# A quarter of the first product by Strassen's seven products in blocks 3 to 5 of a retention and PReLU kernel

## The chip, the cores and the metric

The kernel runs on one NeuronCore of one Trainium2 chip. The metric is the device time of one execution in microseconds. The core has five engines with a queue each: TensorE (PE in the profile, its weight loads PEld), VectorE (DVE), ScalarE (ACT), GpSimd (POOL) and SyncE (SP), which here only starts transfers. SBUF is the memory that all of them read; PSUM holds TensorE's results in eight banks of 128 x 512 fp32.

## The reference

Retention first: for 4 batches and 8 heads of width 64, over 768 positions, a state of 64 x 64 per head decays and takes up the outer product of key and value; the output is the query times the state. The outputs, as 3072 tokens of 512 features, then go through two products with a PReLU between them.

```python
gamma = 1.0 - 2.0 ** (-5.0 - np.arange(H))
for t in range(S):
    state = gamma[None, :, None, None] * state + np.einsum('bhd,bhe->bhde', k[:, :, t], v[:, :, t])
    y[:, :, t] = scale * np.einsum('bhd,bhde->bhe', q[:, :, t], state)
x = y.transpose(0, 2, 1, 3).reshape(B * S, H * D)     # 3072 x 512
h = x @ w_in                                          # 3072 x 2048, the first product
g = np.maximum(h, 0.0) + alpha * np.minimum(h, 0.0)
out = g @ w_out                                       # 3072 x 512, the second product
```

## The kernel before

**Units and blocks.** The positions are cut into 24 units of 128 (`NU`), six to a batch. A block is four units, 512 tokens (`TB`), and there are six blocks. The first eight units are handled as four double units by functions whose names begin with `u`; from unit 8 on the plain ones serve. For a unit, k and q are loaded (`load`, SyncE), scaled by powers of gamma to f16 (`scaled`, mostly GpSimd, L139), turned by a transposing transfer (`turn`, SyncE, L164), and v is cast (`cast`). `prep` does the four for one unit. Then TensorE makes `scores` (L236) and `states` (L196) of a pair of units, VectorE masks the scores (`masked`, L250) and sums the states (`sums`, L211 and L217, with a multiply on GpSimd, L219), and TensorE makes the outputs (`out_first`, `out_second`, L295), which ScalarE and VectorE copy to `xT`, the next block's tokens.

**The first product.** `ffn1` (L622) walks over 16 tiles of 128 of the 2048 hidden features. One tile is four matmuls of 128 weights by 512 tokens, k from the four quarters of the 512 features; `w_in_all` and `xT` lie in SBUF as f16. ScalarE takes the relu of the negated sum (`hm`, L631), VectorE adds the alpha part to PSUM's value (L632) and writes `gt`, the activated tile, in f16. `gt` is one buffer, `hps` takes the four banks p0 to p3 in turn. Blocks 0 and 1 use `ffn1_half` (L650, L659, L664) as well, half the tokens at a time.

**The second product.** Block 0 uses plain matmuls (`ffn2_start`, `ffn2`). From block 1 on, `seven` multiplies 2 x 2 quarters by Strassen's scheme in Winograd's form: seven products of 16 matmuls of 256 columns (L789), in the order A00, A01, `gs1`, `gs0`, `gs2`, A11, `gs3`. The sums of the weights are made once (`w_sums`). The sums of the activations are made per block by `g_sums(n, part, which, eng)` (L739), a subtraction or addition of 128 x 1024 f16 with both inputs and the output in SBUF; part 0 covers the first four tiles of each half of the features, part 1 the other four, and `which` runs from 0 to 3. They land in four tiles `gs0` to `gs3`, which block 0 uses as its `gt`. ScalarE keeps partial results (`kept`, L807), VectorE adds them to later ones (L819), SyncE stores.

**The order of the work** is written by hand: every engine runs its instructions in the order in which the program issues them, and waits on semaphores for inputs and for buffers. The two products are generators; `tick(gen, m)` lets m matmuls out, so that other work can be put between them. In a block n from 2 on, TensorE does `ffn1(n)`, scores and states of the next block's first pair, `seven(n)` with `T_OUT1` = 44 matmuls, the first pair's outputs and the second pair's scores and states, `T_OUT2` = 46 matmuls, the second pair's outputs, and the 22 matmuls that are left. GpSimd's `prep` of the next block's units is issued during `ffn1`, and runs as soon as its buffers (`kq`, four of them) are free. Block 1 has its own arrangement in the same loop (`n > 1` else), with `g_sums` of both parts on VectorE ahead of `seven`.

## Time and profile before

| what | value |
|---|---|
| median of three runs | 199.34 us (198.3, 199.36, 199.34) |
| the profiled execution | 198.51 us, of which its span is 196.5 us |
| granted clock of TensorE | full speed in all 40 slices |
| busy: TensorE, VectorE, GpSimd, ScalarE | 97%, 77%, 61%, 50% of the span |
| `ffn1` of a steady block | 13.81 us |
| last matmul to the end of the span | 3 us |

From 17 us to 193 us TensorE has work almost without a gap. The steady blocks are 28.9 us apart. In a timeline of one engine, a row gives start and duration in us (of several instructions together where a count stands behind the tiles), the engine, the line, the operation, output and inputs with shapes, and in brackets the idle time before it with what ended it. In the chain of work, a row is start, duration, engine, tile and line.

### The profile page before, as it was taken

Reading aid. Unit: us, or ns where it says so; the run is one execution under the profiler, and the core shown is the slowest. Engines: PE = TensorE matmul, PEld = TensorE weight load, DVE = VectorE, ACT = ScalarE, POOL = GpSimd, SP = SyncE. Lnnn points to the kernel's source line nnn. Section 1 sums busy time; section 2 is a strip of 40 time slices with the busy share of each in tenths; the row PEclk is TensorE's granted clock in tenths of the full one; section 3 lists DMA queues with packets and bytes.
Section 4 is the critical chain, followed back from the end, with each engine's and each line's share of the span. In section 5 each row is a group of like instructions: output and inputs, shape, how many; then the busy total and the mean of one; then the engine's idle time right before and its main releaser. Section 6 shows DMA issues by size and latency. Waiting matters only on the chain.

```text
span 196.5 us, 6280 instructions
## 1 busy us (share of the span) xinstructions
PE 190.3 (97%) x2632; PEld 128.9 (66%) x2632; DVE 151.1 (77%) x259; ACT 98.5 (50%) x192; POOL 119.8 (61%) x134
## 2 busy tenths in 40 slices
PE   7988999999999999999999999999999999999993
PEld 5757544558668888644888544888544888444882
DVE  2597989164989998589988589976689985789913
ACT  3378663238677925466333467234476234566110
POOL 3378989999999276994097992197971290040000
PEclk9999999999999999999999999999999999999999
DMA  5999999999998499999999999982660011300014
GB/s 157 330 358 389 407 388 329 337 332 206 209 226 188 89 291 219 226 295 257 213 228 208 286 171 251 253 208 78 180 141 0 3 57 55 109 0 3 0 53 160
DMA packets 92746, 38.75 MB, mean 197 GB/s; under 512 B 70176, under 2 KB 88624, under 8 KB 92720
## 3 DMA queue, kind: packets, MB, share of 16 engines
q1 hardware_dynamic: 91440, 37.36, 74.1%
q10 hardware_dynamic: 1280, 1.01, 1.6%
q8 instruction: 20, 0.33, 0.7%
q14 instruction: 6, 0.05, 0.1%
HBM read 27.35 MB, written 6.29 MB: 171 GB/s over the span
## 4 chain that ended last, share of the span: by engine, by line
PE 81%; DVE 9%; SPq 2%; DMA 2%; POOL 2%; issue 1%; ACT 1%; POOLq 0%
PE hps L622 33%; PE ops L789 28%; PE ops L717 5%; PE hps L650 5%; DVE gt L664 4%; SPq L342 2%; DMA qu<-in_q_dram 2%; DVE gs L739 2%; PE ops L686 2%; PE ya L524 1%; POOL gs L739 1%; PE ya L295 1%; DVE um L496 1%; PE yb L295 1%; PE sca L236 1%
## 5 line engine op out<-in xcount | busy, mean ns | idle before, releaser
L622 PE MATMUL hps<-xT,win 128*128 128x512 f16 x304 | 66.4, 379 | 0.0
L632 DVE SCALAR_TENSOR_TENSOR gt<-hm,small,hps 128x512 f16<-128x512 f32 x76 | 55.4, 745 | 8.6 <-ACT hm L631 3.5
L631 ACT ACTIVATE hm<-hps 128x512 f32<-128x512 f32 x76 | 45.4, 597 | 27.5 <-PE hps L622 27.5
L622 PEld LDWEIGHTS <-win 128*128 128x128 f16 x304 | 29.7, 98 | 34.8
L789 PEld LDWEIGHTS <-gs 128*128 128x128 f16 x320 | 30.9, 98 | 4.2 <-DVE gs L739 0.3
L139 POOL TENSOR_TENSOR kq<-kqs,tab 128x512 f16<-128x512 f32 x30 | 30.7, 1047 | 0.5 <-DMA kqs<-in_k_dram 0.3
L789 PE MATMUL ops<-wsum,gs 128*128 128x256 f16 x240 | 27.9, 273 | 0.1
L219 POOL TENSOR_TENSOR t<-ss,tab 128x256 f16<-128x256 f32 x13 | 8.4, 644 | 28.6 <-DVE ss L217 28.6
L789 PEld LDWEIGHTS <-gt 128*128 128x128 f16 x240 | 22.7, 98 | 3.4 <-DVE gt L632 0.3
L739 POOL TENSOR_TENSOR gs<-gt 128x1024 f16<-128x1024 f16 x7 | 14.9, 2130 | 14.7 <-DVE gt L632 14.7
L807 ACT ACTIVATE kept<-ops 128x512 f32<-128x512 f32 x15 | 9.0, 597 | 23.3 <-PE ops L789 23.3
L664 DVE SCALAR_TENSOR_TENSOR gt<-hm,small,hps 128x256 f16<-128x256 f32 x40 | 17.1, 476 | 4.3 <-ACT hm L659 4.2
L819 DVE TENSOR_TENSOR os<-ops,kept 128x512 f32<-128x512 f32 (+1 forms) x17 | 10.6, 626 | 11.3 <-ACT kept L807 6.3
L789 PE MATMUL ops<-wout,gt 128*128 128x256 f16 x160 | 18.5, 273 | 0.0
L650 PE MATMUL hps<-xT,win 128*128 128x256 f16 x160 | 18.3, 273 | 0.0
L650 PEld LDWEIGHTS <-win 128*128 128x128 f16 x160 | 15.4, 98 | 2.4
L659 ACT ACTIVATE hm<-hps 128x512 f32<-128x512 f32 x20 | 11.9, 599 | 5.7 <-PE hps L650 4.0
L739 POOL TENSOR_TENSOR gs<-gt,gs 128x1024 f16<-128x1024 f16 x5 | 10.6, 2129 | 3.9 <-DVE gs L739 3.9
L717 PE MATMUL ops<-wout,gt 128*128 128x512 f16 x48 | 11.4, 380 | 0.0
L394 ACT ACTIVATE ukT<-trb 128x512 f16<-128x512 f16 (+1 forms) x7 | 4.5, 657 | 11.6 <-PE trb L385 11.6
L789 PE MATMUL ops<-wsum,gt 128*128 128x256 f16 x80 | 10.2, 273 | 0.0
L356 POOL TENSOR_TENSOR ukq<-ku,tab 128x512 f16<-128x512 f32 x6 | 6.1, 1042 | 5.9 <-DMA ku<-in_k_dram 5.9
(107 smaller groups left out, 268.7 us busy)
## 6 DMA issues: line engine op xcount, KB each, us to landing
out_dram<-os SPq DMA_DIRECT2D x20, 256.0 KB, 3.2
wi<-in_moe_w_in_dram SPq DMA_DIRECT2D x8, 512.0 KB, 7.7
wo<-in_moe_w_out_dram SPq DMA_DIRECT2D x8, 512.0 KB, 8.7
kqs<-in_k_dram SPq DMA_DIRECT2D x16, 256.0 KB, 4.3
kqs<-in_q_dram SPq DMA_DIRECT2D x16, 256.0 KB, 4.4
vs<-in_v_dram SPq DMA_DIRECT2D x16, 256.0 KB, 4.6
ku<-in_k_dram SPq DMA_DIRECT2D x4, 256.0 KB, 4.2
qu<-in_q_dram SPq DMA_DIRECT2D x4, 256.0 KB, 4.6
```

Source lines behind the costliest of these rows:

```text
L139: eng.tensor_tensor(out=kqs[u][:, a].rearrange("p i r d -> p r i d"), in0=staged[u][nm].rearrange("p (r i) d -> p r i d", i=4), in1=tab[:, ...
L622: nc.tensor.matmul(out=hps, lhsT=w_in_all[:, hp, 128 * ft : 128 * ft + 128], rhs=xT[n][:, :, hp, :], start=(hp == 0), stop=(hp == 3),)
L631: nc.scalar.activation(out=hm, in_=hps, func=RELU, bias=0.0, scale=-1.0)
L632: nc.vector.scalar_tensor_tensor(out=gt_at(n, ft, slice(0, TB)), in0=hm, scalar=oma_sb[:, ft : ft + 1], in1=hps, op0=MULT, op1=ADD,)
L650: nc.tensor.matmul(out=hps[:, 256 * (ft - f0) : 256 * (ft - f0) + 256], lhsT=w_in_all[:, hp, 128 * ft : 128 * ft + 128], rhs=xT[n][:, half ...
L659: nc.scalar.activation(out=hm, in_=hps, func=RELU, bias=0.0, scale=-1.0)
L664: nc.vector.scalar_tensor_tensor(out=gt_at(n, f, to), in0=hm[:, at], scalar=oma_sb[:, f : f + 1], in1=hps[:, at], op0=MULT, op1=ADD,)
L717: nc.tensor.matmul(out=banks[tq], lhsT=gt_at(n, ft, slice(128 * tq, 128 * tq + 128)), rhs=w_out_all[:, ft, :], start=(ft == 0), stop=(ft = ...
L739: eng.tensor_tensor(out=out, in0=a, in1=b, op=op)
L789: nc.tensor.matmul(out=bk[:, 256 * t : 256 * t + 256], lhsT=a[:, f, 128 * t : 128 * t + 128], rhs=w[:, f, :], start=first and f == 0 and ( ...
L807: nc.scalar.activation(out=t, in_=bank, func=COPY, bias=0.0, scale=1.0)
L819: nc.vector.tensor_tensor(out=os_sb[:, at], in0=x[at.start // 256][:, at], in1=y[:, at], op=op)
```

## The change

A quarter of the first product, that is four of the 16 feature tiles (0, 1, 8 and 9) over all 512 features and 512 tokens, is made by Strassen's seven products in blocks 3, 4 and 5. `ffn1_mix` issues 19 steps, in the order of `MIX`: 12 full tiles as before and seven parts of four matmuls of 256 columns. The parts share three PSUM banks (a, b, c); ScalarE copies intermediate sums out (`kept`), VectorE adds a second bank to them (`add`), and the PReLU of three of the four result quarters is made from SBUF by ScalarE's relu and two GpSimd operations (`ends`). The fourth quarter is finished by VectorE from PSUM.

The parts need four sums of weights, 128 x 1024 f16 each, made once (`win_sum`): two on VectorE behind the outputs of double unit 2, two on GpSimd ahead of block 1's loop, just behind `scaled(11, "q")`. They need four sums of tokens per block, 128 x 512 f16 (`x_sum`): two on VectorE, two on GpSimd, when the tokens are complete.

`gs2` and `gs3` are not made in tiles of their own any more: `g_sums` 2 overwrites the second half of `gt`'s first eight tiles, and `g_sums` 3 the first half of its last eight, which the second product of `seven` reads before. The tiles that this frees hold `win_sum` and `x_sum`. In blocks 3 to 5 `gs0` of part 0 is made by GpSimd, `gs2` of part 0 behind it.

The units of the blocks after block 3 are scaled sooner, during the `seven` of the block before the one that used to scale them: of three units, ScalarE takes k of two (eight instructions each) and GpSimd the rest; the fourth follows at the start of the mixed block. ScalarE casts v. `turn` allocates its own tile. `T_OUT1` goes from 44 to 46, and the calls of `g_sums` move as shown.

```diff
-    T_OUT1, T_OUT2 = 44, 46
+    T_OUT1, T_OUT2 = 46, 46
...
-            uv[w] = sbp.tile([128, 2, 4, 2, D], F16, tag="uv", bufs=2, name=f"uv{w}")
+            uv[w] = sbp.tile([128, 2, 4, 2, D], F16, tag="uv", bufs=3, name=f"uv{w}")
...
         elif which == 2:
-            minus(eng, sm[2][:, f], gt[:, f, t0], gt[:, f, t1])
+            minus(eng, gt[:, f, t1], gt[:, f, t0], gt[:, f, t1])
         else:
-            minus(eng, sm[3][:, f], gt[:, f8, t0], sm[1][:, f])
+            minus(eng, gt[:, f8, t0], gt[:, f8, t0], sm[1][:, f])
...
+    def win_sum(i, eng):
+        if not wins:
+            wins.append(sbp.tile([128, 2, 2, 512], F16, tag="gs2", bufs=1, name="wins0"))
+        if i == 2:
+            wins.append(sbp.tile([128, 2, 2, 512], F16, tag="ukq", bufs=2, name="wins1"))
...
+        minus(eng, wins[i // 2][:, i % 2], x, y, op=op)
...
+    MIX = [(0, 1), (0, 2), 0, (0, 5), (0, 6), 0, (0, 7), 0, 0, (0, 4), (0, 3)] + 8 * [0]
...
+            if i in (1, 6, 7):
...
+                nc.scalar.activation(out=t, in_=bk[r, "b"], func=COPY, bias=0.0, scale=1.0)
+                h[r, i] = t
+            if i in (2, 7, 3):
+                add(r, {2: 1, 7: 7, 3: 6}[i], at if i != 7 else "c")
+            if i == 4:
+                b = bk[r, "b"]
+                prelu(r, relu(b, "hm"), b, 1, 0)
...
+        def ends():
...
+                hm = relu(h[r, i], "uv")
...
+                nc.gpsimd.tensor_tensor(
+                    out=hv,
+                    in0=hv,
+                    in1=oma_sb[:, f : f + 2].unsqueeze(2).to_broadcast([128, 2, 256]),
+                    op=MULT,
+                )
+                nc.gpsimd.tensor_tensor(
+                    out=gt_at(n, slice(f, f + 2), slice(256 * half, 256 * half + 256)),
+                    in0=hv,
+                    in1=v,
+                    op=ADD,
+                )
...
+        for s, step in enumerate(steps):
+            at_step[0] = s
+            yield from part(*step) if step else full()
+            if later and s - later[0][0] >= (3 if later[0][2] == 1 else 2):
+                ends()
+            if s == len(steps) - 4:
+                g_sums(n, 0, 0, nc.gpsimd if rounds == 1 else nc.vector)
+            if s == len(steps) - 2:
+                g_sums(n, 0, 1, nc.vector)
+        g_sums(n, 0, 2, nc.gpsimd)
...
     uoutputs(2, shared=True)
+    win_sum(0, V)
+    win_sum(1, V)
...
     cast(11, A)
+    win_sum(2, G)
+    win_sum(3, G)
...
+        elif n > 2:
+            gen = ffn1_mix(n, MIX, 1)
+            tick(gen, 8)
+            flush(late_stores)
+            if more:
+                scaled(u0 + 3, "k", G)
+                scaled(u0 + 3, "q", G)
+                turn(u0 + 3)
+            for u in range(u0 + UB, min(u0 + 2 * UB, NU)):
+                load(u)
...
             if n > 1:
-                chain(pa, pq, (1, 2), None)
+                chain(pa, pq, [(1, 2, G)])
                 tick(gen, T_OUT1)
+                g_sums(n, 0, 3, G)
+                for u in nxt[0:1]:
+                    scaled(u, "k", A)
             else:
-                g_sums(n, 1, 3, nc.gpsimd)
                 tick(gen, 33)
-                chain(pa, pq, None, None)
+                g_sums(n, 1, 3, G)
+                chain(pa, pq)
...
-            tick(gen, T_OUT2 if n > 1 else 29)
+            tick(gen, 6)
+            for u in nxt[0:2]:
+                cast(u, A)
+            for u in nxt[1:2]:
+                scaled(u, "k", A)
+                scaled(u, "q", G)
+                turn(u)
+            for u in nxt[2:3]:
+                scaled(u, "k", G)
+                scaled(u, "q", G)
+            tick(gen, T_OUT2 - 6 if n > 1 else 23)
             out_first(pb, z=[ps("za"), ps("zb")])
             out_second(pb)
+            for u in nxt[2:3]:
+                turn(u)
+            tick(gen, 7)
+            if n > 1:
+                x_sum(n + 1, 0)
+                x_sum(n + 1, 1)
+                x_sum(n + 1, 2, G)
+                x_sum(n + 1, 3, G)
```

More of the change, by code (lines that the diff above doesn't have):

```diff
@@ L766, in g_sums @@
             gsum[n] = [
-                sbp.tile([128, HF, 256], F16, tag=f"gs{i}", bufs=1, name=f"gs{n}{i}") for i in range(4)
+                sbp.tile([128, HF, 256], F16, tag=f"gs{i}", bufs=1, name=f"gs{n}{i}") for i in range(2)
             ]
@@ L842, in seven @@
         yield from product(c, sm[0], wsum[0], True)
-        yield from product(b, sm[2], wsum[2])
+        yield from product(b, A(1, 0), wsum[2])
         u3 = kept(b, "um1")
@@ L851, in seven @@
         if end:
[L852 removed]
+            gen = product(c, A(0, 1), W(1, 1))
             for _ in range(HF):
```

171 lines of the change are left out of this document (139 added, 32 removed).

## The prediction

> **What bounds the kernel now.** I read the page's totals and its chain first, then the chain in order of time, then the timelines of single engines where the change puts work.
>
> ```profile
> span 196.5 us, 6280 instructions
> PE 190.3 (97%) x2632; PEld 128.9 (66%) x2632; DVE 151.1 (77%) x259; ACT 98.5 (50%) x192; POOL 119.8 (61%) x134
> PE 81%; DVE 9%; SPq 2%; DMA 2%; POOL 2%; issue 1%; ACT 1%; POOLq 0%
> L139 POOL TENSOR_TENSOR kq<-kqs,tab 128x512 f16<-128x512 f32 x30 | 30.7, 1047 | 0.5 <-DMA kqs<-in_k_dram 0.3
> ```
>
> ```profile
> 47.00 3.60 PE hps L650 x32
> ...
> 138.21 13.81 PE hps L622 x64
> ...
> 158.82 5.13 PE ops L789 x46
> ```
>
> TensorE sets the time: 190.3 of 196.5 us busy, 81% of the chain. In the steady blocks the chain is one row of 64 matmuls of 512 columns after another (0.216 us each) and then groups of 256 columns (46 in 5.13 us, 0.1115 each). So a stall of TensorE is lost for good, and work of another engine costs nothing until TensorE waits for it. The question is therefore how close each wait is, and that depends on how VectorE and GpSimd get on side by side. The timelines (start, duration, engine, line, operation) show it:
>
> ```profile
> 31.26 2.04 POOL L356 TENSOR_TENSOR ukq<-ku,tab 128x512 f16<-128x512 f32 x2 [0.37 <-DMA ku<-in_k_dram]
> 33.26 3.02 POOL L356 TENSOR_TENSOR ukq<-qu,tab 128x512 f16<-128x512 f32 x2
> 88.61 2.13 POOL L739 TENSOR_TENSOR gs<-gt 128x1024 f16<-128x1024 f16 x1
> 103.54 0.62 POOL L219 TENSOR_TENSOR t<-ss,tab 128x256 f16<-128x256 f32 x1
> 156.39 2.13 POOL L739 TENSOR_TENSOR gs<-gt 128x1024 f16<-128x1024 f16 x1
> ```
>
> ```profile
> 32.36 2.02 DVE L739 TENSOR_TENSOR wsum<-wout 128x2048 f16<-128x2048 f16 x1
> 90.29 1.00 DVE L739 TENSOR_TENSOR gs<-gt 128x1024 f16<-128x1024 f16 x1
> 92.53 0.68 DVE L739 TENSOR_TENSOR gs<-gs,gt 128x1024 f16<-128x1024 f16 x1
> 103.60 1.11 DVE L739 TENSOR_TENSOR gs<-gt,gs 128x1024 f16<-128x1024 f16 x1
> 156.26 0.68 DVE L250 TENSOR_TENSOR m<-scb,mi 128x512 f16<-128x512 f32 x1
> ```
>
> A VectorE sum with both inputs in SBUF takes 0.68 us where GpSimd is idle (92.53). The one at 90.29 ends at 91.29, 0.55 after the GpSimd operation that ended at 90.74; the one at 103.60 ends at 104.71, 0.55 after GpSimd's 104.16. It works the other way too: the VectorE sum at 32.36 got in between two GpSimd operations, ended at 34.38, and GpSimd's next pair took 3.02 us where 2.04 is usual. At 156.26 an operation with one input in PSUM takes 0.68 beside a running GpSimd operation. So these two kinds exclude each other: whoever is late waits for the other's whole instruction, then VectorE needs 0.55. The PReLU operations, with one input in PSUM, are of the free kind. A GpSimd sum of 1024 columns holds VectorE up to 2.13 us.
>
> **The gain on TensorE.** In each of blocks 3, 4 and 5, 16 matmuls of 512 columns (16 x 0.216 = 3.45 us) give way to 7 products of 4 matmuls of 256 columns. For these the nearest row is L650, the same weights at 256 columns: 32 in 3.60, 0.1125 each, 28 x 0.1125 = 3.15. That is 0.30 us per block; by the 0.1115 of L789, 0.33. Three blocks: -0.9 (bounds -0.9 and -1.0). Nothing else leaves TensorE, so -1.0 is the most that can be won, about 0.5% of the kernel, which is also about what a measurement can tell from no change.
>
> **The weight sums, first pair, on VectorE.** These come behind unit 2's outputs.
>
> ```profile
> 43.60 2.13 POOL L739 TENSOR_TENSOR wsum<-wout,wsum 128x1024 f16<-128x1024 f16 x1
> 45.68 1.17 POOL L916 CAST wout<-wo 128x512 f16<-128x512 f32 x2
> 47.00 1.66 DVE L664 SCALAR_TENSOR_TENSOR gt<-hm,small,hps 128x256 f16<-128x256 f32 x4 [2.54 <-ACT hm L659]
> 55.28 2.47 DVE L696 TENSOR_TENSOR os<-os,ops 128x512 f32<-128x512 f32 x4
> 55.42 0.24 PE ya L524 x2
> ```
>
> VectorE idles 2.54 us before 47.00. The first sum overwrites the tile that block 0's second product reads until 44.88, finds GpSimd at work until 45.73, and ends at 46.28. GpSimd's cast then runs to 46.86, and the second sum ends at 47.4: 0.4 after the PReLU could have begun. From 47.00 to 55.28 VectorE has no idle time, and what ends there, a mask, lets TensorE go on at 55.42. So TensorE loses 0.4 (bounds 0, if the second sum slips in before the cast, and 0.5). GpSimd is pushed by twice 0.55, 1.1 us; its queue is full to 64 us, with 0.18 to spare.
>
> **The second pair, on GpSimd.** It stands behind `scaled(11, "q")`, waits for nothing, and falls on VectorE's four sums for block 1.
>
> ```profile
> 64.27 1.04 POOL L139 TENSOR_TENSOR kq<-kqs,tab 128x512 f16<-128x512 f32 x1 [0.18 <-DMA kqs<-in_q_dram]
> 69.22 2.13 POOL L739 TENSOR_TENSOR gs<-gt,gs 128x1024 f16<-128x1024 f16 x1 [3.91 <-DVE gs L739]
> ```
>
> ```profile
> 66.34 0.68 DVE L739 TENSOR_TENSOR gs<-gt 128x1024 f16<-128x1024 f16 x1
> ...
> 68.39 0.69 DVE L739 TENSOR_TENSOR gs<-gs,gt 128x1024 f16<-128x1024 f16 x1
> ```
>
> ```profile
> 65.40 3.67 PE L789 MATMUL ops<-wout,gt 128*128 128x256 f16 x32
> 68.99 3.22 PE L789 MATMUL ops<-wsum,gs 128*128 128x256 f16 x28
> ```
>
> GpSimd is idle 3.91 us there, which is what the pair (2 x 2.13) seems to fill for nothing. But VectorE's sums are now at 66.7 and GpSimd starts its pair at 66.2 (65.3 if its delay is absorbed). Whichever alternates, two GpSimd sums and four VectorE sums have to go one after another: 66.2 + 4.26 + 0.55 + 3 x 0.65 = 73.0 for the last one, where it ended at 69.08. TensorE's third product needs the first half of `gs1` at 68.99 and the second half four matmuls later, at 69.44; with the 0.4 from above 69.8. It stalls 73.0 - 69.8 = 3.2 us, less some 0.1 for overlap: 3.1 (bounds 2.2, with the earlier start, and 3.3). If the cover were perfect it would be 0, which the third rival takes.
>
> **Block 2.** `gs2` becomes an overwrite of `gt`'s second half, so GpSimd's sum waits for VectorE's reading of it, moves from 88.61 to about 91.0 and now collides with the VectorE sum at 92.53 (+0.5). VectorE's PReLU of the last tiles is then about 0.1 behind TensorE: 0.1 (0 to 0.2).
>
> **The mixed blocks, from their first matmul (0).** Per block ScalarE gets 3 copies more; VectorE has 12 PReLUs, 2 half ones and 3 adds for its 16 PReLUs; GpSimd gets 6 operations for three quarters' PReLU, one more `gs` sum, and two sums of tokens.
>
> ```profile
> 152.05 0.60 ACT L631 ACTIVATE hm<-hps 128x512 f32<-128x512 f32 x1 [0.27 <-PE hps L622]
> 150.69 2.74 DVE L632 SCALAR_TENSOR_TENSOR gt<-hm,small,hps 128x512 f16<-128x512 f32 x4
> 154.20 0.69 DVE L739 TENSOR_TENSOR gs<-gs,gt 128x1024 f16<-128x1024 f16 x1
> 154.81 0.41 DVE L211 TENSOR_TENSOR t<-t,sta 128x256 f16<-128x256 f16 x1
> 157.59 0.15 PE ya L295 x2
> ```
>
> TensorE issues parts of 0.45 and full tiles of 0.863: the part that closes the last sum ends at 6.6, the last tile at 13.5 (13.8 before). VectorE: the last add (`add`, one PSUM input, 0.65) at 9.0; its seven next PReLUs at 0.685 end at 14.05, paced at the last by ScalarE. ScalarE's relu of that add ends at 9.65. GpSimd turns it into `gt` with a multiply and an add (1.05 each by L139, no row has both inputs as f32 tensors; by twice the bytes up to 2.1): 11.8, and then makes `gs0` (2.13): 14.0. Only then can VectorE's `gs1` begin, at 14.1. GpSimd's next instruction, `gs2` in place, is ready at the same moment. If VectorE goes first, GpSimd runs 14.7 to 16.8, VectorE's next SBUF sum waits for it and the last ends at 18.1; sums and masks take 2.05 more: 20.15. The second product reads the last tile early enough, but the outputs that need the masks are due 46 matmuls into `seven`, at 14.16 + 5.13 = 19.3: a stall of 0.9. In block 5, without states, `seven` starts at 13.5, the fifth tile of `gs1` is due at 17.5: a stall of 0.6. If GpSimd goes first, the last PReLU stands behind `gs1` until 17.3, the second product stalls, and it is 1.5, 1.5 and 1.25, 4.25 in all. I take the first, by the row at 32.36, where the waiting VectorE operation came ahead of GpSimd's next: 0.9 + 0.9 + 0.6 = 2.4 (bounds 1.5, with every step 0.3 earlier, and 4.25). The Trainium skill (SBUF — State Buffer, "Who interferes with whom") says that issue order decides, and that the one who issues first holds the shared ports for its whole instruction; the rows above agree on the holding. By that rule GpSimd, whose queue holds `gs2` while VectorE is still in its seventh PReLU until 14.05, goes first, and the whole sum would be 205.5 in place of 203.6.
>
> The rest costs nothing: moving scaling to ScalarE gives it some 6.4 us per `seven`, where it was busy 5 of 15, after the copies that TensorE needs; the loads go behind one transpose on SP's queue, and are used over 8 us later; `gs3` in place waits for the second product and is needed sixty matmuls on; the four sums of the tokens collide with scaling, but are due 1.7 us into the next block. Were that cover gone, each late tile would cost its lateness, once per block.
>
> **The sum.** 198.51 (the profiled execution; 196.5 its span, 2.0 around it) - 0.9 + 0.4 + 3.1 + 0.1 + 2.4 = 203.6. The median shown, 199.34, stands 0.83 above that execution; on its footing 204.4. I take 204.0.
>
> **The rivals.** *One: the collisions cost nothing that TensorE sees*, since GpSimd's sums land in other gaps: then only the matmuls count, 198.51 - 0.9 = 197.6, or 198.4 on the median's footing. For it: before, TensorE waits for VectorE hardly anywhere, and the first products give slack. Against: the slack at 68.99 is 0.4 us. It decides if VectorE's last sum of block 1 ends before 69.8. *Two: only the weight sums pay*; the mixed blocks' outputs are 2 matmuls later, which hides the lateness: 203.6 - 2.4 = 201.2. *Three: only the mixed blocks pay*: 198.51 - 0.9 + 2.4 = 200.0. *Four: GpSimd goes first in the mixed blocks*, because its next instruction is ready at 14.0 and VectorE is busy until 14.05: 203.6 - 2.4 + 4.25 = 205.5. For it: the order of those two times; against: they differ by less than the working can tell, and the row at 32.36. *Five: GpSimd becomes the bound*: an add of two f32 tensors takes 2.1, `gs0` ends 2.6 later, three blocks x 2.6 on top: 211.4.
>
> **How the numbers follow.** My forecast 0.28, rival one 0.25, two 0.17, three 0.08, four 0.15, five 0.07. The forecast's own range is 201.2 to 206.7: its lower bounds and the gain of 1.0 on the profiled footing, the upper ones on the median's. Leaving out rival five and the lower part of rival one, the range is 198.0 to 206.8. Faster by over 0.5% is part of rival one: 0.17. Within 0.5%: the rest of it and part of three: 0.12. Slower: 0.71.
>
> **What would show it.** Right: in block 1 VectorE's four sums stretch from 2.7 to over 5 us with GpSimd's two between them, and TensorE has a gap of 2 us or more early in `seven`; gaps of 0.6 to 1.5 us before the outputs of the next units or in the second product of blocks 3 to 5; mixed stages of 13.5 us. Wrong: VectorE's sums at 0.68 beside GpSimd's 2.13, no gap in TensorE after 65 us, or GpSimd's pair finished before 66 us.

## The result, and the profile after

The changed kernel takes 209.51 us in the median of four runs (205.74 to 211.61), the kernel before 199.02 beside it: it is slower, by a ratio of 1.0396 with a 95% interval of 1.0289 to 1.0502. Run a second time, on another occasion, it gave 1.027 (1.017 to 1.0369). The prediction said slower, 204.0, with a range of 198.0 to 206.8, so the direction was right and the size was not. The ratio is taken from the two of the four executions in which TensorE kept its full clock (205.74 and 207.85); in the other two (211.18, which is the profiled one, and 211.61) it ran some microseconds at half its clock behind a long wait, and so it did in both traces of the changed kernel that are shown here.

The totals of the page after:

```profile
span 209.5 us, 6435 instructions
PE 192.1 (92%) x2668; PEld 132.2 (63%) x2668; DVE 167.8 (80%) x267; ACT 113.4 (54%) x241; POOL 153.6 (73%) x151
PEclk9999999999589999999999999999999999999999
PE 34%; DVE 23%; POOL 19%; DMA 9%; SPq 6%; issue 5%; ACT 2%; POOLq 0%; DVEq 0%
```

TensorE had 81% of the chain and now has 34%; VectorE and GpSimd together went from 11% to 42%. VectorE is busy 16.7 us longer (167.8 for 151.1), and a good part of that is time in which an instruction of it stands and waits for GpSimd: in the last experiment below (e12), where the sums of `w_in` are left out and the two meet far less, it is busy 154.7. The third line shows TensorE's clock in 40 slices, two of them at 5 and 8 tenths.

To place the loss I cut each trace at VectorE's first mask after 30 us, at the first `hps` matmul of each block's first product, and at the last sum into `os`. The time between these marks, in us:

| kernel | to block 2 | block 2 | block 3 | block 4 | block 5 |
|---|---|---|---|---|---|
| before | 40.52 | 28.94 | 28.94 | 28.94 | 26.49 |
| after | 49.54 | 29.34 | 29.67 | 29.73 | 26.90 |
| after, second profile | 49.27 | 29.24 | 29.58 | 29.72 | 26.89 |

Of the 11.35 us between the marks, 9.0 lie ahead of block 2, where the four sums of weights are made, 0.4 in block 2, 1.9 in the mixed blocks. (Another 1.2 lie ahead of the first mark; in the second profile that mark comes 0.2 earlier than in the kernel before, so they are no part of the change.)

Pair 1 are the two sums of `w_in` on VectorE, pair 2 the two on GpSimd. For pair 1, timelines of VectorE and GpSimd (start, duration, engine, line, operation), then TensorE's wait and its next matmuls, then windows of 5 us (busy time of TensorE, its weight loads, VectorE, ScalarE and GpSimd, then the granted clock, the share of the DMA and its GB/s):

```profile
46.13 5.98 DVE L733 TENSOR_TENSOR wins<-win 128x1024 f16<-128x1024 f16 x1 [0.46 <-PE ops L710]
52.15 2.49 DVE L733 TENSOR_TENSOR wins<-wins,win 128x1024 f16<-128x1024 f16 x1
```

```profile
45.14 2.12 POOL L733 TENSOR_TENSOR wsum<-wout,wsum 128x1024 f16<-128x1024 f16 x1
47.21 1.16 POOL L1071 CAST wout<-wo 128x512 f16<-128x512 f32 x2
48.34 2.12 POOL L733 TENSOR_TENSOR wsum<-wout 128x1024 f16<-128x1024 f16 x1
50.41 1.16 POOL L1071 CAST wout<-wo 128x512 f16<-128x512 f32 x2
51.65 2.44 POOL L733 TENSOR_TENSOR wsum<-wout,wsum 128x1024 f16<-128x1024 f16 x1
```

```profile
55.47 3.59 PE L643 MATMUL hps<-xT,win 128*128 128x256 f16 x16 [5.41 <-DVE gt L657]
```

```profile
50.00:55.00 5.00, 0.06 (x1) 0.00 (x0) 4.96 (x4) 0.00 (x0) 4.92 (x5) 0.75 0.97 218
55.00:60.00 5.00, 4.53 (x51) 3.13 (x52) 4.17 (x12) 1.79 (x3) 5.00 (x5) 0.57 0.94 213
60.00:65.00 5.00, 4.92 (x62) 2.71 (x61) 5.00 (x11) 3.80 (x12) 2.42 (x4) 1.00 0.09 21
```

VectorE's first sum stands 5.98 us. GpSimd runs through five instruction ends at its usual pace, 2.12 for a sum and 0.58 for a cast; only ahead of the third sum does VectorE get in, and ends 0.55 later, at 52.11. The second sum then waits for that third sum, to 54.09 + 0.55. Behind the two stands a PReLU that empties a bank, so TensorE waits 5.41 us. After that 16 matmuls take 3.59 us, 0.224 each instead of 0.1125: the granted clock is 0.57 between 55 and 60. The stretch at half clock reaches from 52.50 to 59.33, and TensorE was at work in 3.86 us of it, so it costs some 1.9 us more. These 1.9 us are only a part of the 3.3 to 5.4 between this execution and the two at full clock, so the wait itself may be shorter in those; no trace shows it.

Block 1's sums and the end of a mixed block, VectorE then GpSimd:

```profile
74.81 0.68 DVE L733 TENSOR_TENSOR gs<-gt 128x1024 f16<-128x1024 f16 x1
75.52 2.50 DVE L733 TENSOR_TENSOR gs<-gs,gt 128x1024 f16<-128x1024 f16 x1
...
134.14 0.69 DVE L733 TENSOR_TENSOR gs<-gs,gt 128x1024 f16<-128x1024 f16 x1 [0.28 <-POOL gs L733]
135.52 1.84 DVE L733 TENSOR_TENSOR gs<-gt 128x1024 f16<-128x1024 f16 x1
```

```profile
72.78 2.13 POOL L733 TENSOR_TENSOR wins<-win 128x1024 f16<-128x1024 f16 x1
74.87 2.60 POOL L733 TENSOR_TENSOR wins<-win,wins 128x1024 f16<-128x1024 f16 x1
...
131.97 2.13 POOL L733 TENSOR_TENSOR gs<-gt 128x1024 f16<-128x1024 f16 x1
134.18 2.63 POOL L733 TENSOR_TENSOR gt<-gt 128x1024 f16<-128x1024 f16 x1
```

Pair 2 meets only one of the four sums (2.50 in place of 0.68), because here VectorE's four sums begin 7.7 us later than in e1 below, which has no pair 1, and GpSimd's pair only 6.3 us later. In block 3 the sum at 135.52 waits for GpSimd's in-place sum (`gs2`, which overwrites `gt`). VectorE's second sum had come 0.04 us ahead of that one, at 134.14, as the prediction took it; it had stood idle for 0.28 us.

### The profile page after: what moved, and what is told of

Same layout as the page of the kernel before. It is cut to its first block, busy times and chain, and to the rows that moved or that the text cites. A ratio compares the mean times of both kernels' runs of the same rounds, so it can differ in the third digit from the quotient of the medians.

```text
span 209.5 us, 6435 instructions
## 1 busy us (share of the span) xinstructions
PE 192.1 (92%) x2668; PEld 132.2 (63%) x2668; DVE 167.8 (80%) x267; ACT 113.4 (54%) x241; POOL 153.6 (73%) x151
## 4 chain that ended last, share of the span: by engine, by line
PE 34%; DVE 23%; POOL 19%; DMA 9%; SPq 6%; issue 5%; ACT 2%; POOLq 0%; DVEq 0%
PE ops L783 15%; DVE gs L733 8%; DMA ku<-in_k_dram 5%; DMA wi<-in_moe_w_in_dram 4%; DVE gt L657 4%; PE hps L615 4%; SPq L335 4%; PE hps L908 3%; POOL kq L138 3%; POOL gs L733 3%; DVE wins L733 3%; POOL gt L1001 3%; POOL gt L733 3%; POOL hm L995 2%; POOL ukq L349 2%
## 5 line engine op out<-in xcount | busy, mean ns | idle before, releaser
L783 PEld LDWEIGHTS <-gt 128*128 128x128 f16 x400 | 38.2, 98 | 5.8 <-DVE gt L625 0.5
L908 PE MATMUL hps<-xT,win 128*128 128x512 f16 x144 | 33.0, 379 | 0.0
L917 DVE SCALAR_TENSOR_TENSOR gt<-hm,small,hps 128x512 f16<-128x512 f32 x36 | 26.0, 744 | 4.1 <-ACT hm L901 3.1
L783 PE MATMUL ops<-wout,gt 128*128 128x256 f16 x240 | 28.1, 273 | 0.2 <-DVE gt L625 0.2
L901 ACT ACTIVATE hm<-hps 128x512 f32<-128x512 f32 x39 | 23.2, 595 | 7.5 <-PE hps L908 6.7
L615 PE MATMUL hps<-xT,win 128*128 128x512 f16 x112 | 24.6, 379 | 0.0
L908 PEld LDWEIGHTS <-win 128*128 128x128 f16 x144 | 14.1, 98 | 14.4
L625 DVE SCALAR_TENSOR_TENSOR gt<-hm,small,hps 128x512 f16<-128x512 f32 x28 | 20.6, 745 | 3.1 <-ACT hm L624 0.9
L624 ACT ACTIVATE hm<-hps 128x512 f32<-128x512 f32 x28 | 16.7, 597 | 9.8 <-PE hps L615 9.1
L783 PE MATMUL ops<-wsum,gs 128*128 128x256 f16 x160 | 19.7, 273 | 2.3 <-DVE gs L733 2.2
L643 PEld LDWEIGHTS <-win 128*128 128x128 f16 x160 | 16.1, 103 | 8.8 <-DVE gt L657 5.7
L783 PE MATMUL ops<-wsum,gt 128*128 128x256 f16 x160 | 19.1, 273 | 0.1
L615 PEld LDWEIGHTS <-win 128*128 128x128 f16 x112 | 10.9, 98 | 12.9 <-POOL win L1071 0.4
L652 ACT ACTIVATE hm<-hps 128x512 f32<-128x512 f32 x20 | 11.8, 598 | 12.8 <-PE hps L643 6.6
L733 POOL TENSOR_TENSOR gt<-gt 128x1024 f16<-128x1024 f16 x7 | 16.4, 2343 | 3.0 <-DVE gs L733 2.8
L783 PEld LDWEIGHTS <-gs 128*128 128x128 f16 x160 | 14.9, 98 | 5.4 <-DVE gs L733 3.6
```

Of the source, the lines that this page charges most:

```text
L615: nc.tensor.matmul(out=hps, lhsT=w_in_all[:, hp, 128 * ft : 128 * ft + 128], rhs=xT[n][:, :, hp, :], start=(hp == 0), stop=(hp == 3),)
L624: nc.scalar.activation(out=hm, in_=hps, func=RELU, bias=0.0, scale=-1.0)
L625: nc.vector.scalar_tensor_tensor(out=gt_at(n, ft, slice(0, TB)), in0=hm, scalar=oma_sb[:, ft : ft + 1], in1=hps, op0=MULT, op1=ADD,)
L643: nc.tensor.matmul(out=hps[:, 256 * (ft - f0) : 256 * (ft - f0) + 256], lhsT=w_in_all[:, hp, 128 * ft : 128 * ft + 128], rhs=xT[n][:, half ...
L652: nc.scalar.activation(out=hm, in_=hps, func=RELU, bias=0.0, scale=-1.0)
L733: eng.tensor_tensor(out=out, in0=a, in1=b, op=op)
```

## The experiments

The theory to be tested: sums of two SBUF tensors on VectorE and instructions of GpSimd exclude each other, and each such meeting ahead of TensorE costs its wait. The rivals: VectorE is starved by something else; the meetings are not the loss; or the loss is the clock.

**The ports by themselves (m1).** A kernel of its own with eight rows; five sums on GpSimd, one on VectorE is the first.

> A kernel of its own, which leaves out the whole computation and stores zeros; GpSimd runs rows of five 128x1024 f16 sums (2.13 us each), and one VectorE operation begins beside the first of them. Theory (VectorE is passed over as long as GpSimd's next instruction is ready): VectorE's sum of two SBUF tensors takes 9 us or more beside independent sums (row 1), 3.5 us or more beside independent casts of 0.58 us (row 5), and under 2.8 us beside sums that each wait for the one before (row 2). Rival (the ports change hands at every instruction's end, as the prediction had it): under 2.8 us in all three, under 1.2 us in row 5. Both: 0.7 us or less with one input in PSUM (row 3) and alone (row 7). Row 4 turns it round, five sums on VectorE and one on GpSimd: by the theory, if it holds for both engines, GpSimd's sum takes 4 us or more, by the rival under 3. Row 6 has a VectorE copy of one tensor, row 8 GpSimd sums that each wait for something done long before: open.

```profile
3.24 2.65 DVE L57 TENSOR_TENSOR r<-x,y 128x1024 f16<-128x1024 f16 x1 [0.76 <-DVE y L47]
14.41 2.58 DVE L57 TENSOR_TENSOR r<-x,y 128x1024 f16<-128x1024 f16 x1 [8.52 <-issue]
25.75 0.69 DVE L57 TENSOR_TENSOR r<-acc,x 128x512 f16<-128x512 f32 x1 [8.76 <-issue]
47.12 2.31 DVE L129 COPY r<-x 128x1024 f16<-128x1024 f16 x1 [1.80 <-issue]
57.73 0.68 DVE L57 TENSOR_TENSOR r<-x,y 128x1024 f16<-128x1024 f16 x1
```

Beside GpSimd's five sums VectorE's takes 2.65 us, which is the rest of one GpSimd sum and 0.55; where GpSimd's sums wait for each other 2.58; alone 0.68; with an input in PSUM 0.69 beside GpSimd. A copy of one SBUF tensor is held up too (2.31). So the exclusion is as the prediction read it, and in these rows the ports change hands at each end: VectorE's sum beside casts took 0.68 us, and turned round, GpSimd's sum beside five of VectorE's took 2.45. Starving as a rule is out; the 5.98 us are not explained by it.

**Without pair 1 (e1).** Two memsets of VectorE take the place of its two sums.

```diff
-    win_sum(0, V)
-    win_sum(1, V)
+    for i in range(2):
+        nc.vector.memset(wins[0][:, i], 0.0)
```

> Leaves out the first pair of weight sums (VectorE writes zeros into their tile, which reads nothing). Theory (the first pair costs the most, TensorE's wait of 5.4 us and the half clock behind it): median 201 to 203.5 us, clock 1.0, no wait of TensorE over 0.5 us between 45 and 57 us. Rival (the first pair costs 0.4 us, as predicted, and the time went elsewhere): 205 us or more.

206.15 us beside 199.66 for before, ratio 1.0233 (1.0147 to 1.0319), where the theory said 201 to 203.5. The time lies in the rival's range, but not for the rival's reason: pair 1's wait is gone, and pair 2 now meets VectorE in full:

```profile
67.09 2.11 DVE L733 TENSOR_TENSOR gs<-gt 128x1024 f16<-128x1024 f16 x1
69.24 2.49 DVE L733 TENSOR_TENSOR gs<-gs,gt 128x1024 f16<-128x1024 f16 x1
```

```profile
71.79 0.61 PE L783 MATMUL ops<-wsum,gs 128*128 128x256 f16 x4 [1.97 <-DVE gs L733]
73.12 5.30 PE L783 MATMUL ops<-wsum,gs 128*128 128x256 f16 x24 [0.72 <-DVE gs L733]
```

The two waits make 2.69 us; the prediction had 3.1 for this pair, with 2.2 as the lower bound. But the 24 matmuls behind them take 5.30 us, 0.22 each, twice what they take at full clock. This second part of the price was in no term of the sum.

**The clock (e7).** e1 with 18 matmuls on zeros, 2.0 us of work that nobody needs, ahead of that third product.

```diff
+        if n == 1:
+            z = bank(k + 2, "wps")
+            for _ in range(18):
+                nc.tensor.matmul(
+                    out=z[:, 0:256], lhsT=wz[:, 0:128], rhs=wz[:, 0:256], start=True, stop=True
+                )
```

> The kernel without pair 1 (memsets; wrong weights), which took 206.2, with 18 matmuls of 256 columns on zeros (2.0 us of work that nobody needs) ahead of block 1's third product, where TensorE waited 1.97 us. Theory: the wait of VectorE's sums costs twice, once as the wait and once as some 5 us of TensorE at half its granted clock behind it; with TensorE kept at work the wait is the same but the clock stays near 1.00, and the 24 matmuls that took 5.30 us take 2.7: 203.0 to 204.5, 2 to 3 faster though more is done. Rival: the low clock has another cause (it comes with the next load, or is of that execution alone); then the time is 206 to 208 and the 24 matmuls still take over 5 us.

```profile
69.68 2.13 PE L832 MATMUL wps<-wz 128*128 128x256 f16 x18
71.64 0.60 PE L783 MATMUL ops<-wsum,gs 128*128 128x256 f16 x4
73.72 2.79 PE L783 MATMUL ops<-wsum,gs 128*128 128x256 f16 x24 [1.48 <-DVE gs L733]
```

In the profile the 24 matmuls take 2.79 us, and from the first mask to block 2 it takes 44.62 us instead of e1's 45.93. In time it is 204.96 beside 200.84, ratio 1.0205 (1.0125 to 1.0284); e1's 1.0233 lies within that interval, so the gain in time is not settled. All four executions of e7 have a mean clock of 0.997 to 1.0, where three of e1's four have 0.983 to 0.992; that work on TensorE always keeps the clock is not shown. The Trainium skill (TensorE: Matmul & The Clock Gate, "Part 1: The HAM clock gate") says that the gate goes to half after an idle window of some 3.4 us, and that this window is free-running. The lengths agree: the stretch at half clock is 6.8 us in the profiles of after and e1 and 3.4 in the second one of the changed kernel. The idle time does not: e1 lost the clock after waits of 1.97 and 0.72 us with four matmuls between them, which is no whole window, and here the measurement decides. e11, below, waited 0.54 and 2.64 us at this place and kept 1.00.

**Without all four sums (e2).**

```diff
-    win_sum(0, V)
-    win_sum(1, V)
+    for i in range(2):
+        nc.vector.memset(wins[0][:, i], 0.0)
...
-    win_sum(2, G)
-    win_sum(3, G)
+    for i in range(2):
+        nc.vector.memset(wins[1][:, i], 0.0)
```

> Leaves out all four sums of weights (zeros written by VectorE). What is left against the kernel before are the mixed blocks and the overwriting sums. Theory: 1 to 2 us below the run without the first pair alone, 200 to 202 us, and still above the kernel before, since the mixed blocks cost about 1 us each where they were to win 0.3. Rival (the second pair costs 3.1 us, as predicted): 3 us below it, at or under the kernel before.

203.02 us, ratio 1.0187 (1.0097 to 1.0276). To block 2 it takes 41.50, 1.0 above before, in which two memsets of 0.5 us stand ahead of block 1's sums; the blocks behind take 2.4 more than before (29.48, 29.58, 29.73, 26.88). So the four sums with their waits and the low clock behind them are worth about 8 of the 9 us ahead of block 2, and the mixed blocks pay on their own. The largest waits left on TensorE for VectorE (us in total, number, longest); of the first row 0.57 us stand in block 1 and 0.79 in block 5:

```profile
PE ops L783 <- DVE gs L733: 1.4, 2, 0.8
PE ya L288 <- DVE m L243: 1.1, 4, 0.3
```

**Letting VectorE in (e3).** Everything is computed; a two-column copy on GpSimd, of pair 1's second sum, stands ahead of GpSimd's casts.

```diff
     w_sums(1, G, [0])
+    nc.gpsimd.tensor_copy(out=gwait[:, 0:2], in_=wins[0][:, 1, 1, 510:512])
     cast_w("wo", 3, [G, G])
```

> Computes everything. One small GpSimd copy of VectorE's second sum is put ahead of GpSimd's casts, so that GpSimd has to wait until the first pair is done. Theory (VectorE is starved only while GpSimd's next instruction is ready): the first pair ends by 47.5 us, TensorE's wait of 5.4 us shrinks to under 1 us, GpSimd is 1.5 us later, median 201.5 to 204 us although a wait was added. Rival (the sum itself, or its buffer, is slow): the pair still takes over 5 us, and the kernel is not faster than the changed one.

210.72 us, ratio 1.0549 (1.0491 to 1.0608): the expectation, which had no second meeting in it, was missed by over 6 us. Pair 1 behaves:

```profile
47.58 1.68 DVE L733 TENSOR_TENSOR wins<-win 128x1024 f16<-128x1024 f16 x1 [0.46 <-PE ops L710]
49.29 0.69 DVE L733 TENSOR_TENSOR wins<-wins,win 128x1024 f16<-128x1024 f16 x1
```

and VectorE, now in time, meets both of pair 2's sums:

```profile
71.63 2.60 DVE L733 TENSOR_TENSOR gs<-gt 128x1024 f16<-128x1024 f16 x1
74.27 2.48 DVE L733 TENSOR_TENSOR gs<-gs,gt 128x1024 f16<-128x1024 f16 x1
```

```profile
75.00:80.00 5.00, 3.19 (x16) 2.32 (x17) 4.67 (x7) 0.41 (x1) 3.91 (x3) 0.66 1.17 262
```

TensorE waits 4.0 us for these at once, and its clock falls to 0.66. The wait moved from the one pair to the other.

**Is the 5.98 chance? (the changed kernel again)**

> The changed kernel once more. In its first profile VectorE's first sum of pair 1 took 5.98 us, past five ends of GpSimd instructions, and TensorE waited 5.4 us and ran the next 3.6 us at half its clock. Theory A: that is fixed by what stands in the two queues there; then it is seen again: a first sum of over 5 us, a wait of TensorE of over 4.5 us at that place, a granted clock of about 0.57 between 55 and 60 us, and a time of 207 to 212. Rival B: it was the chance of one execution; then the first sum takes 2.7 us or less, TensorE waits at most 2.5 us there, and the time is 203 to 206.

208.21 us beside 200.84; its profile shows it again, at the same place in GpSimd's queue. TensorE waits 3.95 us for it, less than the 4.5 expected, as it had waited 1.36 for something else just before, and the clock is 0.88 and 0.78 in the two windows:

```profile
44.69 5.95 DVE L733 TENSOR_TENSOR wins<-win 128x1024 f16<-128x1024 f16 x1 [0.46 <-PE ops L710]
```

```profile
54.00 3.47 PE L643 MATMUL hps<-xT,win 128*128 128x256 f16 x16 [3.95 <-DVE gt L657]
```

So it is not the chance of one execution. Two more kernels of single instructions tried to copy it: GpSimd's order of that place (m2), and VectorE's sum coming into a GpSimd queue that has run for 5 or 9 us (m3).

> A kernel of its own (the whole computation is left out, zeros are stored): GpSimd runs the order that it has where pair 1 lies, a sum of 1024 columns, two casts, a sum, two casts, a sum of the first sum, and VectorE brings its two sums of SBUF tensors into the first of these; row 2 behind a cast out of PSUM and a release by TensorE, rows 3 and 4 with loads and ScalarE's copies running. Theory A: this order alone keeps VectorE out until GpSimd has to wait; the first sum takes over 4.5 us in row 1. Theory B: the ports change hands at each instruction's end; at most 2.7 us in all rows, and the 5.98 us stay unexplained. Theory C: loads or ScalarE's work matter; long in rows 3 or 4 alone.

> A kernel of its own (the whole computation is left out, zeros are stored). GpSimd runs ten independent sums of 1024 columns, or four of them and then its order of pair 1; VectorE first does operations with their input in PSUM, so that its sum of two SBUF tensors comes when GpSimd has been at work for about 5 or 9 us. Theory A (backlog): GpSimd asks for the ports ahead of time for instructions that wait for nothing, so a VectorE sum that comes into a queue which has run for long stands behind several of them; rows 1, 2 and 3 then show a sum of over 4 us, row 5 five of them. Theory B: at the next end of an instruction VectorE gets in however long GpSimd has been at work; at most 2.7 us everywhere, and the 5.98 us of the changed kernel stay unexplained. Theory C: only beside ScalarE's copies, TensorE and loads; long in row 3 alone.

Neither did. In m2 the first sums took 2.31, 1.14, 2.58 and 0.88 us, in m3 every sum that met GpSimd got in at the next end; five of VectorE's against ten of GpSimd's simply alternate:

```profile
84.09 12.03 DVE L57 TENSOR_TENSOR r<-w 128x1024 f16<-128x1024 f16 x5
```

One row says nothing: in m3's third, the one with ScalarE's copies and loads, VectorE's sum came when GpSimd was done. In m2 loads (third row, 2.58) and ScalarE's copies (second row, 1.14) made no difference; work of TensorE beside the sums is in no row, so whether it matters is not tested.

Two edits of the changed kernel itself then ask what in the queue decides. e10: a two-column copy of GpSimd's own first sum behind that sum, so that GpSimd waits for itself there. e11: GpSimd's second sum and its first two casts change places.

```diff
     w_sums(1, G, [0])
+    nc.gpsimd.tensor_copy(out=gown, in_=wsum[1][:, 3, 254:256])
     cast_w("wo", 3, [G, G])
     w_sums(2, G, [0])
```

```diff
     w_sums(1, G, [0])
-    cast_w("wo", 3, [G, G])
     w_sums(2, G, [0])
     cast_w("wo", 3, [G, G])
+    cast_w("wo", 3, [G, G])
```

> The changed kernel with one tiny GpSimd copy of two columns of its first sum of w_out right behind that sum, so that GpSimd waits for its own predecessor there (all else is computed as before). In the changed kernel VectorE's first sum of pair 1 got the ports only ahead of the GpSimd sum that waits for its own predecessor, in both profiles. Theory A: VectorE gets in where GpSimd has to wait for itself; now that is at the first end, the first sum takes 1.5 to 1.9 us instead of 5.98, the second at most 1.5, TensorE's wait there falls from 4.0 or more to under 1.5 us with no low clock behind it; VectorE is then earlier at block 1's sums and loses up to 2.5 us there again: 204 to 207. Rival B: the own wait is not what lets VectorE in; the first sum still takes over 4 us, and the time is that of the changed kernel, 206 to 210.

> The changed kernel, and only GpSimd's second sum of w_out and its first two casts change places, so that GpSimd's order where pair 1 lies is sum, sum, four casts, sum. Theory A (own wait): VectorE still gets in only ahead of the last of these sums, at the same time as before: a first sum of 5.5 to 6.2 us. Theory C (the casts keep VectorE out, sums do not): it gets in at the end of the first sum, 1.5 to 1.9 us. Theory D (a set number of instructions is let through, whatever they are): as A or up to 1 us off, which this run does not tell from A.

VectorE in e10, then in e11, then GpSimd in e11:

```profile
47.16 2.68 DVE L733 TENSOR_TENSOR wins<-win 128x1024 f16<-128x1024 f16 x1 [0.46 <-PE ops L710]
49.87 1.10 DVE L733 TENSOR_TENSOR wins<-wins,win 128x1024 f16<-128x1024 f16 x1
```

```profile
46.23 1.66 DVE L733 TENSOR_TENSOR wins<-win 128x1024 f16<-128x1024 f16 x1 [0.46 <-PE ops L710]
47.92 2.49 DVE L733 TENSOR_TENSOR wins<-wins,win 128x1024 f16<-128x1024 f16 x1
```

```profile
45.21 2.13 POOL L733 TENSOR_TENSOR wsum<-wout,wsum 128x1024 f16<-128x1024 f16 x1
47.29 2.58 POOL L733 TENSOR_TENSOR wsum<-wout 128x1024 f16<-128x1024 f16 x1
```

Both let VectorE in at the first end: e10 by GpSimd's own wait, e11 without one, with a sum in the place of a cast. So an own wait is enough but not needed, and in this place, as far as the one execution of e11 shows, it matters that a cast follows. It is no rule of casts: in e10 VectorE's second sum got in between two of them (49.87, 1.10), and in m2 at the end of a sum that a cast follows. What decides stays open. Neither edit pays: e10 takes 210.14 where 204 to 207 was expected, ratio 1.0488 (1.0415 to 1.056), since VectorE is in time for pair 2 again and TensorE waits 3.7 us at once there; e11's single run gave 208.00, with a wait of 2.64 there.

**The in-place sum in the mixed blocks (e4, then e6 and e8).** e4 is e2 with GpSimd's in-place sum of the first quarter put off until behind the states' sum in blocks 3 and 4, and given to VectorE in block 5.

```diff
-        g_sums(n, 0, 2, nc.gpsimd)
...
-                chain(pa, pq, [(1, 2, G)])
+                chain(pa, pq, [(1, 2, G)] if n == 2 else [(0, 2, G), (1, 2, G)])
```

> The kernel without the four sums of W_in (memsets in their place; so the mixed blocks compute with wrong weights), which took 203.0, and in blocks 3 and 4 GpSimd's in-place sum of the first quarter stands behind the next states' sum instead of right behind its first sum; in block 5 it is VectorE's. Theory: the mixed blocks lose their time because that in-place sum on GpSimd holds VectorE's second sum for a whole instruction; 0.7 to 1.1 us per block come back, 200.3 to 201.3. Rival: the mixed blocks are late because the chain of GpSimd's multiply, add and first sum is late whatever stands behind it; then the time stays within 0.6 of 203.0.

203.27 beside 200.84, ratio 1.0143 (1.0086 to 1.0201) against e2's 1.0187; block 3 took 29.58 as before the edit, block 4 30.31, block 5 26.22. Only where the sum left GpSimd did 0.66 come back. In blocks 3 and 4 it now stands ahead of GpSimd's multiply for the next state, for which VectorE idles 2.58 us (139.40), and that late state holds TensorE's next outputs (0.24 and 0.17 us in block 3, where e2 waits 0.19 and 0.34 at its masks). Then two kernels that compute everything, with the four sums of weights on GpSimd in block 2 behind its scaling. e8 has the mixed blocks as in the change, e6 gives the in-place sum to VectorE there, right behind its second sum (in block 5 behind the others). The diff goes from e8 to e6.

```diff
                 g_sums(n, 0, 1, nc.vector)
-        g_sums(n, 0, 2, nc.gpsimd)
+                if n + 1 < NBLK:
+                    g_sums(n, 0, 2, nc.vector)
...
         if not more:
+            g_sums(n, 0, 2, V)
             g_sums(n, 1, 2, V)
```

> The whole computation. All four sums of W_in are GpSimd's, in block 2 behind its scaling (ScalarE makes block 2's four copies of v instead); VectorE's second sum of block 2 stands behind its last PReLU and the in-place sums of block 2 are VectorE's, behind the first output of seven(2); in blocks 3 and 4 the first in-place sum is VectorE's, right behind its second sum, in block 5 behind the others. Theory: what the change loses are the places where a VectorE sum and a GpSimd sum meet ahead of TensorE; with blocks 1 and 2 as before (80.2 at the start of block 2's first product when the first mask is at 39.6) and 0.3 won and at most 0.3 lost in each mixed block, the ratio to the kernel before is 0.995 to 1.006. Rival: the waits only move, as they did in the last two variants, to block 2's masks or to the mixed blocks' outputs; 1.010 to 1.025.

> The whole computation, the four sums of W_in and block 2 as in the kernel just described, but the mixed blocks 3, 4 and 5 as in the changed kernel. Theory: against it the mixed blocks lose 0.4 to 0.8 us each by the in-place sum on GpSimd: 1.2 to 2.2 us more, a ratio to the kernel before of 1.005 to 1.015. Rival: who makes the in-place sum does not matter there: the same time within 0.6.

204.40 and 205.96 beside 201.73; ratios 1.016 (1.0087 to 1.0233) and 1.0266 (1.0203 to 1.033). The mixed blocks take 29.56, 29.19, 26.22 in e6 and 30.11, 29.73, 26.89 in e8: 0.55, 0.54 and 0.67 for who makes the in-place sum, 1.76 together, as the theory said. But block 2 takes 32.60 and 32.25, 3.3 to 3.7 more than before. In e6 the moved sums keep VectorE's second sum (2.06 us), and so the masks, late (TensorE waits 0.48 and 0.53 us), and VectorE's in-place sums meet GpSimd's (3.32 us for two, a wait of 0.79). There the rival was right.

**The sums in GpSimd's gaps (e9), and no sums of `w_in` (e12).** e9 puts two sums into gaps that GpSimd showed in block 1, two behind block 2's scaling, and gives all four first in-place sums to VectorE. e12 is e9 with zeros written by ScalarE in the place of the sums, and block 2's copies of v back on GpSimd.

```diff
+    win_sum(0, G)
     w_sums(3, G, [0])
     w_sums(3, G, [1])
+    win_sum(1, G)
     scaled(11, "q", G)
...
-            g_sums(n, 0, 2, G)
+            win_sum(2, G)
+            win_sum(3, G)
+            g_sums(n, 0, 2, V)
```

> The whole computation, with the four sums of W_in on GpSimd in places where its trace shows it idle and VectorE's work there has its input in PSUM: the first ahead of its last sums of w_out (idle 2.58 us before them in the changed kernel), the second ahead of the scaling of the last unit (idle 2.80 us), the other two behind block 2's scaling, with block 2's copies of v on ScalarE; the first in-place sums of blocks 2 to 5 are VectorE's. Theory: with no VectorE sum and GpSimd sum meeting ahead of TensorE, block 1 takes what it took before (80.2 at the start of block 2's product when the first mask is at 39.6), block 2 28.9 to 29.3, blocks 3 to 5 29.5, 29.2 and 26.2 as in the variant just run: 0.3 to 1.2 above the kernel before, a ratio of 1.001 to 1.007. Rival: the waits move again, by over 1 us in block 1 or 2: 1.010 or more.

> The four sums of W_in are left out (ScalarE writes zeros to their tiles in block 2, so the mixed blocks compute with wrong weights), and the first in-place sums of blocks 2 to 5 are VectorE's; else the changed kernel. Theory: the sums of W_in and the in-place sums on GpSimd are the whole loss; from the first mask on, block 1 takes 40.5 to 41.0, block 2 28.9 to 29.3, blocks 3 to 5 29.0, 29.2 and 26.2, together at most 0.8 above the kernel before, a ratio of 0.997 to 1.005: also with every sum for nothing the change would win next to nothing. Rival 1: without any meeting of the two engines the gain of three times 0.3 us is there: 0.992 to 0.997. Rival 2: something else of the change (the scaling moved sooner, ScalarE's part) costs over 1 us: above 1.006.

e9: 205.85 beside 200.78, ratio 1.0176 (1.0083 to 1.0269). The rival won: the gaps had been left by the waits, and with pair 1 gone GpSimd's queue closes up and its second sum meets VectorE's four again (TensorE waits 0.60 and 1.57 us):

```profile
67.72 2.50 DVE L733 TENSOR_TENSOR gs<-gs,gt 128x1024 f16<-128x1024 f16 x1
```

```profile
67.09 2.58 POOL L733 TENSOR_TENSOR wins<-wins,win 128x1024 f16<-128x1024 f16 x1
```

e12: 202.25 beside 200.61, ratio 1.0066 (1.0021 to 1.0111). The middle lies above what the theory allowed (1.005) and where rival 2 begins (1.006), the interval reaches into both, and the profile says where the time is:

| kernel | to block 2 | block 2 | block 3 | block 4 | block 5 |
|---|---|---|---|---|---|
| before | 40.52 | 28.94 | 28.94 | 28.94 | 26.49 |
| e2, no sums | 41.50 | 29.48 | 29.58 | 29.73 | 26.88 |
| e6, sums in block 2 | 41.32 | 32.60 | 29.56 | 29.19 | 26.22 |
| e9, sums in gaps | 43.52 | 31.70 | 29.03 | 29.19 | 26.23 |
| e12, no sums of `w_in`, fewer meetings | 40.47 | 30.28 | 29.03 | 29.19 | 26.50 |

Ahead of block 2 all is as before. Of the 1.34 us in block 2, 1.09 are one wait, in which ScalarE, VectorE and TensorE stand in a row:

```profile
105.38 0.63 ACT L151 ACTIVATE vx<-vs 128x512 f16<-128x512 f32 x1 [1.43 <-DMA vs<-in_v_dram]
105.92 2.00 ACT L130 ACTIVATE kq<-kqs,tab 128x64 f16<-128x64 f32 x8
107.83 0.57 ACT L801 ACTIVATE kept<-ops 128x512 f32<-128x512 f32 x1
```

```profile
108.43 0.69 DVE L813 TENSOR_TENSOR os<-ops,kept 128x512 f32<-128x512 f32 x1 [1.95 <-DMA vs<-in_v_dram]
```

```profile
109.18 1.91 PE L783 MATMUL ops<-wout,gt 128*128 128x256 f16 x16 [1.09 <-DVE os L813]
```

ScalarE, which in the change casts v during `seven`, waits for a load; its copy of a product stands behind that and behind eight scalings. In the changed kernel this wait is not there. It also appears in e4 (1.16) and e9 (0.85), where block 1 is earlier too, but not in e2, whose block 1 is as early and whose casts of v found their load landed. So with the casts on ScalarE, ahead of its copies, TensorE can be held by a load that lands late; in these three profiles that costs about 1 us. No version was found that beats the kernel before.

## Why the prediction was wrong, point by point

**The reading of the ports** was right: m1 has 2.65 beside GpSimd, 0.68 alone and 0.69 with an input in PSUM. The change is slower because of it: without the sums of `w_in` and with the first in-place sums on VectorE (e12) the marks lie 155.47 us apart, in the changed kernel 165.18, before 153.83, so 9.7 of the 11.35 us go with these sums, their meetings and the low clock behind them.

**The gain on TensorE** was sized well: the first product takes 13.51, 13.57 and 13.48 us in blocks 3, 4 and 5 of the second profile of the change, from its first matmul to what follows, where it took 13.90, 13.91 and 13.81: 1.06 against 0.9.

**The first pair is the step that failed**: "So TensorE loses 0.4 (bounds 0, if the second sum slips in before the cast, and 0.5)". It lost 5.41 and 3.95 us at that place in two profiles. The working let VectorE in at the first end of a GpSimd instruction, as in the row at 32.36, its example of VectorE getting in between two. That row showed one case, not a rule: here VectorE was passed over at five ends (5.98 and 5.95 us). The path was another one too: TensorE stood before a PReLU that empties a bank of `hps`, not before the mask that the prediction named. The bounds, 0 and 0.5, came from the same case; the upper one should have been a wait for GpSimd's queue, which the prediction itself read as full to 64 us. What decides who goes first at an end stays open, as e10, e11 and the small kernels show.

**A term was missing**: what a wait of TensorE does to its clock. In the profile of after it is some 1.9 us behind pair 1, in e1 2.5 behind pair 2 (24 matmuls in 5.30 instead of e7's 2.79). The trace of the kernel before keeps its full clock, so it could not price this, but a forecast of a 3-us gap should have named it. (The change is not alone in it: six executions of the kernel before have a mean clock of 0.990 to 0.992.)

**The second pair** was right as a mechanism and near in size where VectorE comes in time: 2.69 us of waiting in e1 for 3.1. In the changed kernel itself it is less (0.54 and 0.72 us), as the first pair's wait had already put VectorE behind.

**Block 2** took 0.3 to 0.4 for 0.1. **The mixed blocks** lost, their gain of 0.3 put back, 1.0, 1.1 and 0.7 us against 0.9, 0.9 and 0.6: 2.8 for 2.4. VectorE went first, as the forecast took it, so rival four did not come about there. The issue order that the Trainium skill (SBUF — State Buffer, "Who interferes with whom") names agrees: VectorE's sum starts at 134.14, GpSimd's at 134.18, and it is 0.04 to 0.05 us ahead in every mixed block of both profiles. VectorE's PReLU ended 14.14 us into the block, where the prediction had 14.05, but GpSimd's in-place sum came at 14.45, where it had 14.0. So the choice came out right for another reason than the row at 32.36, and partly by luck. In the first pair GpSimd did go first, at five ends, although VectorE's sum stood waiting. Rival five is out: the add of two f32 tensors takes 1.27 us, not 2.1.

**"The rest costs nothing"** held in the two profiles of the changed kernel. In three variants (e4, e9, e12) ScalarE's wait for a load of v costs 0.85 to 1.16 us, in e2 nothing.

## What to carry to other kernels

A sum of two SBUF tensors that is moved beside a busy GpSimd is bounded by the queue it may have to stand behind, not by the instruction that it meets first; where the trace shows one meeting, both ends of the range are needed. A gap in an engine's timeline is free only as long as what made the gap stays: the variants that put the same sums elsewhere moved the wait to the next meeting. To a wait of TensorE belongs a possible stretch at half clock behind it: here it followed waits of 3.7 to 5.4 us in four profiles and waits of 2.7 us in all in one (e1), did not follow 3.2 us in all in another (e11), and was worth some 1.9 to 2.5 us where it was worked out.

## What the runs showed of the hardware that was not expected

VectorE's sum was passed over at five ends of GpSimd instructions (5.98 and 5.95 us), with the same kinds of instructions handing over at each end in three small kernels; changing places of one sum and two casts (e11), or one own wait of GpSimd (e10), ended it. TensorE's clock fell to half after waits of 1.97 and 0.72 us with four matmuls between them (e1), and not after 0.54 and 2.64 (e11). A VectorE copy with one SBUF tensor as its only input was held up by GpSimd as well (2.31 us).
